# Turning the gated activations of a mixture of adapters by DMA in pairs, with two moves in the order of the work around it

## The chip, the cores and the metric

The kernel runs on one core of one Trainium2 chip. The metric is the time of one execution on the device in microseconds (us). One execution of each kernel was also recorded by the hardware profiler; its span, from the first to the last instruction of the program, is what the views of the profile divide up.

## The reference

Two layers follow one another. The first is attention with pooled keys; the second sends each row through the best two of eight low-rank adapters and adds the result to the row.

```python
B, N, C = 4, 12288, 128            # q: [4, 12288, 128], kv: [4, 384, 32, 128]
kv_pool = kv.reshape(B, H // 4, 4, W // 4, 4, C).mean(axis=(2, 4))   # 4x4 patches: 768 rows a batch
k = v = kv_pool.reshape(B, -1, C) @ w_sr
s = (q @ k.transpose(0, 2, 1)) / np.sqrt(C)
a = softmax(s)
x = (a @ v).reshape(B * N, C)
logits = x @ w_gate                 # 8 experts
topk = best 2 of 8 by logits;  w = softmax of those two logits
out = x + sum over the two e of  w_e * ((x @ A[e]) @ B[e])      # rank 16 each
```

All of it is fp32 in and out. The 8 adapters of rank 16 fill one 128 x 128 matrix side by side, so that "down" (x @ A) and "up" (@ B) are one 128 x 128 matmul each for 128 rows, with the gate (the weight of each expert, zero for six of the eight) multiplied in between.

## The kernel before

**Tiling.** The 49,152 rows are cut into 96 chunks of 512 rows (NCHUNK), 24 for each batch (NB). Four chunks form a group (GC), for which q comes in once: GpSimd's queue casts the group to bf16 into a buffer in DRAM (`cast_q`, L83), and the Sync engine's queue reads it back transposed (`load_qT`, L92), so that the channels lie on the partitions. The 768 keys of a batch are six tiles of 128 (J).

**What happens to a chunk.**
- `scores` (L309): three units of two key tiles each; two matmuls of 512 columns into `sg`, then one exponential on ScalarE into `em`.
- `attend` (the tile `acc`): for each quarter of 128 rows, six matmuls of `em` against the values. The values carry extra columns, one of them ones, so that the sums of the softmax and the logits come along. There is one buffer of `acc`.
- `normalize` (L330, L338): VectorE takes the reciprocal and multiplies; this makes `xn` and frees `acc`.
- `top` and `route` (L358 to L376) on VectorE and GpSimd, and `gates` (L383 to L386: a tanh on ScalarE, two operations on GpSimd) make the gate weights `gw`, for two chunks at a time in the main part.
- `transposes` (L407): TensorE turns `xn`, and for some chunks the gated activations of another chunk, into one PSUM tile `tt_ps`, which VectorE copies out as `tts`.
- `down` (`h_ps`), `gate` (L439, VectorE, writes `hg`, `h` or `hs`), a transpose of the gated activations, `up` (`d_ps`), and `finish` (L486, VectorE adds `xn`; every second one stores two chunks, L491, on the Sync queue).

**Slots.** The body of the loop over `k` is called a slot here. From slot 13 on, slot `k` computes the scores of chunk `k`, attends chunk `k-1`, normalizes chunk `k-2`, and lets one older chunk `x_` enter down and gate: `enter[k]` is chunk `k-4` in the main part. Every engine runs its instructions in the order in which the loop writes them (`keep`). Slots 0 to 7 are an order written out by hand.

**Three ways of turning the gated activations.** Between gate and up, the activations of a chunk must be transposed.
- By TensorE (`by_pe` and all chunks in no other list): four 128 x 128 transposes (`tt_ps<-id_bf,hg`) in the slot after the gate, and the copy L407 is twice as wide.
- Through the Sync queue (`by_queue`, chunks 9 to 65): `gate_turn` writes the gated tile, and a transposing DMA (L459) turns it; up comes six or seven slots after the gate (`up_slot`). Chunks with k % 4 == 1 go alone (tiles `h1`, `t1`, shown as `t<-h`); chunks with k % 4 == 3 and the next one share a DMA (tiles `hs`, `ht`, four buffers). Chunks with k % 4 == 2 (14, 18, ..., 62), and chunk 10, are left to TensorE.
- By strip (chunks 66 to 89, SOLO and TURN mark the bounds): one DMA (`turn_dma`, L425) turns the rows of one chunk and the gated activations of another. These are the late slots, from 74 on, with an order of their own: two units of scores, down, normalize, gate, then two quarters of `attend` with `up` and `finish` of up to two chunks, and two more quarters.

**Where the Sync queue stands.** A group's `load_qT` is written at the start of slot 4g-6, unless the chunk that enters in this slot is in `by_queue`; then it follows the DMA of `gate_turn`. For groups 6 to 18 that chunk is one with k % 4 == 2.

**Keys of the next batch.** The patches of the second batch are summed by 24 operations on GpSimd (L229 and L227), which `sums.pop(0)()` places at the end of even slots 8 to 20. The steps `keys`, `values` and `turn` of its three thirds are taken from `rest` at slots 14 to 16, 18 to 20 and 21 to 23; `keys` of the last third (tile `kpT_ps`) is in slot 21 and needs all 24.

Of the kernel before, what the change touches and what calls it, by code (L numbers as in the profile page):

```python
# [20 lines left out]
def kernel(  # L21
# [47 lines left out]
    def mm(*a, **k):  # L69
        return keep(nc.tensor.matmul(*a, **k))  # L70
# [240 lines left out]
    def attend(k, s):  # L311
        b = k // NB
        if s == 0:
            acc[k] = ps_a.tile([P, S, 256], FP32, tag="acc", name="acc")
        o = acc[k][:, s, 0:VE]
        for j in range(J):
            mm(o, em[k][:, s, j], vx[b][:, j, 0:VE], start=(j == 0),
               stop=(j == J - 1))
# [25 lines left out]
    SOLO, TURN = NCHUNK - 6, NCHUNK - 28  # L344
# [75 lines left out]
    def narrow(k, t):  # L420
        keep(nc.gpsimd.tensor_copy(strip(t, 0)[:, 0], xn[k][:, :, 0:C]))
# [14 lines left out]
    def gate(k, into=None):  # L436
        k0, m = first[k], k - first[k]
        hg[k] = run.tile([P, S, P], BF16, tag="hg", name="hg") if into is None else into
        keep(nc.vector.tensor_tensor(  # L439
            hg[k].rearrange("p s (e r) -> p (s e) r", e=E),  # L440
            hp[k].rearrange("p s (e r) -> p (s e) r", e=E),
            gw[k0][:, m * S:(m + 1) * S].rearrange("p s e -> p (s e)")
            .unsqueeze(2).broadcast_to([P, S * E, RK]), op=ALU.mult))
# [1 line left out]
    pair = []  # L445

    def gate_turn(k):
        if k % 4 == 1:
            src, dst = (hpool.tile([P, 1, S, P], BF16, tag=tag, name=tag, bufs=3) for tag in ("h1", "t1"))
        elif k % 4 == 3:  # L450
            src, dst = (hpool.tile([P, 2, S, P], BF16, tag=tag, name=tag) for tag in ("hs", "ht"))
            pair[:] = src, dst
        else:
            src, dst = pair
        i = int(k % 4 == 0)
        gate(k, src[:, i])
        hgT[k] = dst[:, i]
        if k % 4 != 3:
            keep(nc.sync.dma_start(dst.rearrange("c h s p -> c (h s) p"),  # L459
                                   src.rearrange("p h s c -> p (h s c)"), transpose=True))  # L460

# [81 lines left out]
    def begin(k):  # L543
        nonlocal sums, rest
        b, i = divmod(k, NB)
        g = k // GC
        if k in casts:
            cast_q(4 + casts.index(k))
        if k in halves:
            g, u = halves[k]  # L550
            cast_q(g, u, u + 4)
        if k in rows_at:
            load_kv(*rows_at[k], None)
        if i == 0 and 0 < b < B - 1:
            rest = prepare(b + 1, nc.gpsimd)[1]
        if k == 3:
            sums, rest = prepare(1, nc.gpsimd)
            sums = sum(sums, [])
        if 3 <= k < 15:
            load_kv(1, (k - 3) // 4, (k - 3) % 4, None)  # L560
        if k == 7:
            for _ in range(2):
                sums.pop(0)()
# [16 lines left out]
        left = [k for k in left if k not in enter[t]]  # L580
        t += 1

    by_queue = [k for k in range(9, TURN - 2) if k % 4 != 2 and k != 10]
    by_strip = range(TURN - 2, SOLO)
    slot = {x_: t for t, xs in enter.items() for x_ in xs}
    taken = [slot[x_] + (3 if x_ in by_strip else 2) for x_ in slot if x_ not in by_queue]
# [7 lines left out]
    by_pe = enter[SOLO - 2][1:]  # L594
# [14 lines left out]
    kh, ku, kd, kdone = [], [], [], []  # L609
# [40 lines left out]
    kh, ku = enter[k1 - 1], enter[k1 - 2]  # L650
    for k in range(k1, NCHUNK):
        b, i = divmod(k, NB)
        ka = att.get(k, [])
        kx = enter.get(k, [])
        begin(k)

        def after_norm(kn):
            top(kn)
            if kn == first[kn] + size[kn] - 1:
                route(first[kn])  # L660

        kn = [n for n in att.get(k - 1, []) if normed[n] == k]
        unit()
        if k in loads and k < TURN + 5 and not any(x_ in by_queue for x_ in kx):
            load_qT(loads[k])
        ku = ku + late_up.pop(k, [])
        if kx and not kd and all(x_ in by_dma for x_ in kx):
            down(kx[0])
            todo = []
            for n in kn:  # L670
                normalize(n)
                if n in by_dma:
                    narrow(n, k)
                    todo = [(xT, n)]
            tanhs()
            for h_ in kh:
                if h_ in by_pe:
                    transposes(None, h_, nc.vector)
            unit()
            gate(kx[0], strip(k, 0)[:, 1])  # L680
            todo.append((hgT, kx[0]))
            if k != SOLO + 2:
                turn_dma(k, *todo)
                if k in loads:
                    load_qT(loads[k])
            for n in range(2):
                if kh and kh[0] in by_pe:
                    attend(ka[0], n)
                if n < len(ku):
                    up(ku[n])  # L690
                    finish(ku[n])
                if not (kh and kh[0] in by_pe):
                    attend(ka[0], n)
            assert len(ku) < 3
            unit()
            for n in kn:
                after_norm(n)
            attend(ka[0], 2)
            for x_ in kx[1:]:
                down(x_)  # L700
                if x_ in by_pe:
                    gate(x_)
                elif k < SOLO - 3:
                    turn_alone(x_)
                else:
                    gate(x_, strip(k, 0)[:, 0])
                    turn_dma(k, (hgT, x_), *todo)
            attend(ka[0], 3)
            for x_ in kx:
                if x_ not in by_pe:  # L710
                    up_at(k + (3 if k < SOLO - 3 else 2), x_)
            kh, ku = [x_ for x_ in kx if x_ in by_pe], [c for c in kh if c in by_pe]
            continue
        tanhs()
        for x_ in kd:
            down(x_)
        todo = []
        for n in kn:
            normalize(n)
            if n in by_dma:  # L720
                narrow(n, k)
                todo.append((xT, n))
        px = [c for c in kx if c not in by_dma]
        ph = [c for c in kh if c not in by_queue and c not in by_strip]
        pairs = [(px[j] if j < len(px) else None, ph[j] if j < len(ph) else None)
                 for j in range(max(len(px), len(ph)))]
        for x_, h_ in pairs[:1]:
            transposes(x_, h_, nc.vector)
        for x_ in kd:
            gate(x_)  # L730
        unit()
        for u_ in ku:
            up(u_)
            finish(u_)
        for a_ in ka[:-1]:
            for s in range(S):
                attend(a_, s)
            normalize(a_)
            after_norm(a_)
        if ka and len(ka) == 1:  # L740
            attend(ka[0], 0)
        for n in kn:
            after_norm(n)
        for x_ in kx[:1]:
            down(x_)
        if k >= 13:
            unit()
            n0 = 1
        else:
            attend(ka[0], 1)  # L750
            n0 = 2
        for x_ in kx[:1]:
            if x_ in by_queue:
                gate_turn(x_)
                up_at(up_slot[x_], x_)
                if k in loads:
                    load_qT(loads[k])
            elif x_ in by_strip:
                gate(x_, strip(k, 0)[:, 1])
                turn_dma(k, *todo, (hgT, x_))  # L760
                todo = []
                up_at(k + 3, x_)
            elif k == NCHUNK - 1:
                turn_alone(x_)
                up(x_ - 1)
                finish(x_ - 1)
            else:
                gate(x_)
        if todo:
            turn_dma(k, *todo)  # L770
        kd = []
        if rest and i in ((14, 15, 16, 18, 19, 20, 21, 22, 23) if b == 0 else (5, 6, 7, 13, 14, 15, 21, 22, 23)):
            rest.pop(0)()
        for a_ in ka[-1:]:
            for s in range(n0 if len(ka) == 1 else 0, S):
                if s == S - 1:
                    for x_, h_ in pairs[1:]:
                        transposes(x_, h_, nc.scalar)
                        kd = [x_] if x_ is not None else []
                attend(a_, s)  # L780
        ku = [c for c in kh if c not in by_queue and c not in by_strip]
        kh = kx[:1] + kdone
        kdone = kd
        if k % 2 == 0 and 8 <= k <= 20:
            for _ in range(4 if k == 18 else 3):
                sums.pop(0)()
        for w in adds_at.get(k, []):
            add_patches(*w)
# [174 lines left out]
```

## Time and profile before

| what | value |
|---|---|
| three runs | 372.04, 379.13 and 382.07 us; median 379.13 us |
| the profiled execution | 371.5 us, of which the span is 369.7 us |
| TensorE matmul (PE) busy | 358.4 us, 97% of the span |
| VectorE (DVE), ScalarE (ACT), GpSimd (POOL) busy | 292.5, 292.7 and 229.8 us |
| mean granted TensorE clock | 0.999 |
| DMA | 88.08 MB, mean 238 GB/s |

PEld is TensorE's weight load, which overlaps its matmuls; SPq is the Sync engine's queue of DMA issues. In a row of the timeline the first number is the start, the second the time from the first to the last of the merged instructions, then engine, line, operation, out<-in, shapes, and a count; what stands in brackets is the idle time of the engine before the row and what ended it. The profiled execution was shorter than each of the three runs.

### The profile page before, as it was taken

The page shows a single profiled execution, that of the slowest core. Times are in us where ns is not written, and L with a number is a line of the kernel's source. Part 1 is how long each engine was busy: PE and PEld are TensorE (multiplying, and loading weights), DVE is VectorE, ACT ScalarE, POOL GpSimd, SP SyncE. Part 2 cuts the span into 40 slices and gives each one's busy share as a digit, 9 for nine tenths or more (in the row PEclk, how much of TensorE's full clock was granted, in tenths as well). Part 3 has the DMA queues.
Part 4 walks back from the last instruction along what each step waited for, and adds up shares of the span by engine and source line. Part 5 has one row for each costly group of instructions (what it writes and reads, how often), then busy time and mean ns, then how long its engine had stood idle before and what let it go on. Part 6 is the DMA issues. An engine that isn't in the chain of part 4 may idle for free.

```text
span 369.7 us, 11065 instructions
## 1 busy us (share of the span) xinstructions
PE 358.4 (97%) x4266; PEld 281.2 (76%) x4272; DVE 292.5 (79%) x923; ACT 292.7 (79%) x363; POOL 229.8 (62%) x519
## 2 busy tenths in 40 slices
PE   7999999999999999999999999999999999999993
PEld 4767788877787787787787877788787777777782
DVE  1347799887888888888898888888887777679795
ACT  1548986787878888888878878879878999898873
POOL 1110368889878677667758757766666766565442
PEclk9999999999999999999999999999999999999999
DMA  7989769999798999999999999999699999999723
GB/s 246 383 301 222 252 173 278 307 296 230 181 275 198 256 303 286 221 223 330 186 249 282 253 244 223 278 299 238 135 185 224 258 220 202 222 210 208 208 87 156
DMA packets 72869, 88.08 MB, mean 238 GB/s; under 512 B 51345, under 2 KB 51601, under 8 KB 72465
## 3 DMA queue, kind: packets, MB, share of 16 engines
q1 hardware_dynamic: 65728, 62.93, 67.8%
q0 software_dynamic: 6656, 24.12, 28.8%
q8 instruction: 33, 0.54, 0.6%
q10 hardware_dynamic: 432, 0.33, 0.3%
q14 instruction: 20, 0.16, 0.1%
HBM read 50.53 MB, written 36.70 MB: 236 GB/s over the span
## 4 chain that ended last, share of the span: by engine, by line
PE 87%; DMA 4%; DVE 3%; POOL 3%; issue 1%; ACT 1%; SPq 0%; DVEq 0%; ACTq 0%; POOLq 0%
PE acc L70 35%; PE sg L70 31%; PE d_ps L70 5%; PE tt_ps L70 5%; PE h_ps L70 5%; PE kpT_ps L70 2%; DMA kvr<-in_kv_dram 2%; DMA turn<-turn 2%; POOL kvr L229 1%; PE v_ps L70 1%; PE qT_ps L70 1%; PE kfT_ps L70 1%; DVE xn L338 1%; ACT em L309 1%; POOL kvr L227 1%
## 5 line engine op out<-in xcount | busy, mean ns | idle before, releaser
L309 ACT ACTIVATE em<-sg 128x1024 f16<-128x1024 f32 x288 | 283.1, 1022 | 58.0 <-PE sg L70 55.3
L70 PE MATMUL sg<-qT,kfT 128*128 128x512 bf16 x570 | 169.2, 379 | 0.5 <-ACT em L309 0.2
L70 PE MATMUL acc<-vx,em 128*128 128x136 f16 x2280 | 167.5, 223 | 0.3
L70 PEld LDWEIGHTS <-em 128*128 128x128 f16 x2304 | 146.6, 98 | 18.7 <-DVE xn L338 3.0
L338 DVE TENSOR_TENSOR xn<-acc,rinv 128x540 f32<-128x540 f32 x95 | 68.4, 720 | 3.3
L486 DVE TENSOR_TENSOR osb<-d_ps,xn 128x512 f32<-128x512 f32 x92 | 62.8, 688 | 2.4 <-PE d_ps L70 0.5
L541 POOL TENSOR_TENSOR kvr<-kvr 128x512 f32<-128x512 f32 (+1 forms) x48 | 57.0, 1203 | 0.5
L370 POOL TENSOR_TENSOR over<-xn,srt 128x64 f32<-128x64 f32 (+1 forms) x120 | 31.0, 279 | 36.2 <-DVE srt L358 34.4
L385 POOL TENSOR_TENSOR gw<-th,over 128x64 f32<-128x64 f32 (+1 forms) x60 | 17.3, 288 | 48.6 <-ACT th L383 48.1
L70 PEld LDWEIGHTS <-kfT 128*128 128x128 bf16 x576 | 45.2, 98 | 2.7 <-issue 0.6
L330 DVE RECIPROCAL rinv<-acc 128x4 f32<-128x4 f32 x95 | 17.3, 182 | 34.8 <-PE acc L70 32.0
L407 DVE COPY tts<-tt_ps 128x1024 bf16<-128x1024 bf16 (+1 forms) x73 | 36.8, 505 | 0.0
L70 PEld LDWEIGHTS <-xn 128*128 128x128 bf16 x296 | 22.5, 98 | 16.5 <-DVE xn L338 0.2
L358 DVE MAX8 srt<-xn 128x8 f32<-128x8 f32 x380 | 34.5, 153 | 0.1
L70 PEld LDWEIGHTS <-tts 128*128 128x128 bf16 x388 | 27.0, 98 | 7.0 <-DVE tts L407 0.4
L70 PE MATMUL h_ps<-a_bf,tts 128*128 128x128 bf16 x284 | 27.5, 219 | 0.0
L70 PE MATMUL tt_ps<-id_bf,xn 128*128 128x128 bf16 x284 | 27.4, 219 | 0.0
L376 POOL TENSOR_SCALAR over<-over 128x64 f32<-128x64 f32 (+1 forms) x60 | 19.8, 330 | 5.4
L439 DVE TENSOR_TENSOR hs<-h_ps,gw 128x512 bf16<-128x512 f32 x28 | 19.1, 683 | 4.5 <-POOL gw L386 4.0
L229 POOL TENSOR_TENSOR kvr<-kvr 128x512 f32<-128x512 f32 x18 | 22.4, 1270 | 0.1
L439 DVE TENSOR_TENSOR hg<-h_ps,gw 128x512 bf16<-128x512 f32 x26 | 17.9, 688 | 5.8 <-POOL gw L386 5.2
L70 PEld LDWEIGHTS <-turn 128*128 128x128 bf16 x176 | 13.2, 98 | 9.4 <-DMA turn<-turn 0.9
(98 smaller groups left out, 313.8 us busy)
## 6 DMA issues: line engine op xcount, KB each, us to landing
out_dram<-osb SPq DMA_DIRECT2D x46, 512.0 KB, 5.7
kvr<-in_kv_dram POOLq DMA_DIRECT2D x24, 512.0 KB, 6.8
kvr<-in_kv_dram SPq DMA_DIRECT2D x21, 512.0 KB, 7.6
qbf<-in_q_dram POOLq DMA_DIRECT2D x20, 512.0 KB, 6.8
qf<-in_q_dram SPq DMA_DIRECT2D x8, 256.0 KB, 7.5
kvr<-in_kv_dram SPq DMA_DIRECT2D x6, 256.0 KB, 7.5
qbf<-in_q_dram POOLq DMA_DIRECT2D x4, 256.0 KB, 5.5
out_dram<-osb SPq DMA_DIRECT2D x3, 256.0 KB, 2.4
```

Of the source, the lines that this page charges most:

```text
L70: return keep(nc.tensor.matmul(*a, **k))
L229: keep(adder.tensor_tensor(u[:, lo:hi], u[:, lo:hi], v[:, lo:hi], op=ALU.add))
L309: keep(nc.scalar.activation(o, i_, AF.Exp, bias=0.0, scale=scale))
L330: keep(nc.vector.reciprocal(ri, acc[k][:, :, VC]))
L338: keep(nc.vector.tensor_tensor(x[:, :, 0:VC], acc[k][:, :, 0:VC], ri.unsqueeze(2).broadcast_to([P, S, VC]), op=ALU.mult))
L358: keep(nc.vector.max(srt[k0][:, m, s], xn[k][:, s, C:C + E]))
L370: keep(eng.tensor_tensor(d, lg, so[:, :, i].unsqueeze(2).broadcast_to([P, n, 8]), op=ALU.subtract))
L376: keep(eng.tensor_scalar(mask, mask, 0.0, None, op0=ALU.is_ge))
L407: keep(nc.vector.tensor_copy(sb[:, lo:hi], ps[:, lo:hi]))
L439: keep(nc.vector.tensor_tensor(hg[k].rearrange("p s (e r) -> p (s e) r", e=E), hp[k].rearrange("p s (e r) -> p (s e) r", e=E), gw[k0][:, m ...
L486: keep(nc.vector.tensor_tensor(osb[:, int(k == kb)], dp[k], xn[k][:, :, 0:C], op=ALU.add))
L541: keep(nc.gpsimd.tensor_tensor(u, u, v, op=ALU.add))
```

## The change

Three things change. All chunks from 11 to 65 go through the Sync queue, and two neighbours, odd and even, share one transposing DMA; only 9 and 65 go alone. Their up comes seven slots after the gate (six from chunk 56 on), and `load_qT` in slots 18, 22, ..., 66 now follows the DMA of the slot's pair. One of GpSimd's sums moves from slot 18 to slot 16 and one from slot 20 to slot 18. And in the late slots a quarter of `attend` is always written ahead of each `up`.

```diff
     def gate_turn(k):
-        if k % 4 == 1:
+        alone = k % 2 and k + 1 not in by_queue
+        if alone:
             src, dst = (hpool.tile([P, 1, S, P], BF16, tag=tag, name=tag, bufs=3) for tag in ("h1", "t1"))
-        elif k % 4 == 3:
+        elif k % 2:
             src, dst = (hpool.tile([P, 2, S, P], BF16, tag=tag, name=tag) for tag in ("hs", "ht"))
             pair[:] = src, dst
         else:
             src, dst = pair
-        i = int(k % 4 == 0)
+        i = int(k % 2 == 0)
         gate(k, src[:, i])
         hgT[k] = dst[:, i]
-        if k % 4 != 3:
+        if alone or i:
             keep(nc.sync.dma_start(dst.rearrange("c h s p -> c (h s) p"),
                                    src.rearrange("p h s c -> p (h s c)"), transpose=True))
...
-    by_queue = [k for k in range(9, TURN - 2) if k % 4 != 2 and k != 10]
+    by_queue = [k for k in range(9, TURN - 2) if k != 10]
...
             for n in range(2):
-                if kh and kh[0] in by_pe:
-                    attend(ka[0], n)
+                attend(ka[0], n)
                 if n < len(ku):
                     up(ku[n])
                     finish(ku[n])
-                if not (kh and kh[0] in by_pe):
-                    attend(ka[0], n)
...
         if k % 2 == 0 and 8 <= k <= 20:
-            for _ in range(4 if k == 18 else 3):
+            for _ in range(4 if k in (16, 18) else 2 if k == 20 else 3):
                 sums.pop(0)()
```

## The prediction

> **What bounds the kernel now.** I read the page first, then the windows by stage, the groups of TensorE's instructions in the main part, the timeline of two neighbouring slots, and last the Sync queue, GpSimd and the late slots. The page says that TensorE has next to nothing to give away:
>
> ```profile
> span 369.7 us, 11065 instructions
> PE 358.4 (97%) x4266; PEld 281.2 (76%) x4272; DVE 292.5 (79%) x923; ACT 292.7 (79%) x363; POOL 229.8 (62%) x519
> ```
>
> A busy TensorE need not be one that sets the time, so look at starts rather than busy time. Two slots of the main part, the second with the gated activations turned by TensorE:
>
> ```profile
> 169.35 1.23 PE L70 MATMUL acc<-vx,em 128*128 128x136 f16 x18
> ...
> 171.07 0.59 PE L70 MATMUL sg<-qT,kfT 128*128 128x512 bf16 x2
> ...
> 172.73 1.23 PE L70 MATMUL acc<-vx,em 128*128 128x136 f16 x18
> ...
> 174.23 0.39 PE L70 MATMUL tt_ps<-id_bf,xn 128*128 128x128 bf16 x4
> 174.45 0.39 PE L70 MATMUL tt_ps<-id_bf,hg 128*128 128x128 bf16 x4
> 174.68 0.59 PE L70 MATMUL sg<-qT,kfT 128*128 128x512 bf16 x2
> ...
> 176.34 1.23 PE L70 MATMUL acc<-vx,em 128*128 128x136 f16 x18
> ```
>
> From `acc` to `acc` the first slot takes 172.73 - 169.35 = 3.38 us, the second 3.61. The difference, 0.23, is just the time from the `hg` transposes to the next matmul (174.68 - 174.45). So a slot is as long as what TensorE issues in it, and four transposes cost 0.23 us of the end.
>
> **Part 1: 13 chunks leave TensorE.** Chunks 14, 18, ..., 62 are 13, so 52 transposes go. The group in the stretch 100 to 276 us is the thing removed (48 matmuls, which is 12 chunks; the 13th is just ahead of the stretch):
>
> ```profile
> L70 PE MATMUL tt_ps<-id_bf,hg 128*128 128x128 bf16 x48 | 4.6, 219 | 0.0
> ```
>
> Its busy time counts overlapping matmuls twice over; 0.23 for each chunk is the price. For the 12, 12 x 0.23 = -2.8 us; the 13th falls into a stall of part 2 and is counted there. VectorE's copy gets shorter as well, worth nothing while TensorE sets the pace. Bounds: -2.8, and 0 if another engine takes over.
>
> What is added: as many transposing DMAs as before (15 single and 14 pairs become 2 and 27), but 13 more chunks in them. The queues show what this meets:
>
> ```profile
> 124.00:166.00 42.00, 42.00 (x519) 33.28 (x517) 36.57 (x117) 34.44 (x42) 29.63 (x57) 1.00 1.11 258
> ```
> ```profile
> 171.88 3.45 SPq L92 DMA_TRANSPOSE qT<-qbf  x1
> 173.17 0.69 DVE L439 TENSOR_TENSOR hg<-h_ps,gw 128x512 bf16<-128x512 f32 x1 [0.27 <-POOL gw L386]
> ...
> 209.25 1.25 SPq L459 DMA_TRANSPOSE ht<-hs  x1
> ...
> 213.90 7.06 SPq L92 DMA_TRANSPOSE qT<-qbf  x1
> ...
> 234.15 0.59 PE L70 MATMUL sg<-qT,kfT 128*128 128x512 bf16 x2
> ```
> ```profile
> DMA to landing us min/median/max: 3.1/4.0/6.9
> ```
> ```profile
> DMA to landing us min/median/max: 11.7/11.7/11.7
> ```
>
> The last two are the pairs (`ht`), and the load of q issued at 213.90. In the first row the column before the last is the DMA share: 1.11, packets overlapping, no room to see. A pair has 2 chunks and lands at best 3.1 us after its issue, 1.25 of which is the issue: (3.1 - 1.25) / 2 = 0.93 us of the DMA engines for a chunk, an upper estimate. The Sync queue also gets a new order: `load_qT` of groups 6 to 18 stood at the start of the slot and now stands behind the gate and the pair's DMA. In the slot above that gate ended at 173.86, and with 1.25 for the issue the load starts at 175.1 instead of 171.9, 3.2 us later; the next store and pair queue up behind its long issue, but their own users are some slots away. The load at 213.90, the tightest I found, landed at 225.6; its group's first scores start at 234.15, so 8.5 us of cover. Less 3.2, less 0.93 for one more chunk directly ahead, leaves 4.4 us. Up comes six slots after the pair's DMA, about 20 us, against 4 to 7 us for landing; and the four pair buffers come round after eight slots, one slot after the last up that reads them. I take 0 for the DMAs, covered by these 4.4 us; the bounds are 0 and what the second rival works out.
>
> The Trainium skill says in Advanced Engine Details and Errata, X-Bar Transpose (TRN2), that such DMAs run about as fast as plain ones, 350 to 400 GB/s. By that a chunk of 128 KiB would be an estimated 0.35 us, not 0.93, and the DMA side of this change would hardly exist; the row decides.
>
> **Part 2: sums of the second batch.** In slots 16 to 21 GpSimd works without a break:
>
> ```profile
> 82.05 1.27 POOL L229 TENSOR_TENSOR kvr<-kvr 128x512 f32<-128x512 f32 x1
> ...
> 84.97 0.36 POOL L376 TENSOR_SCALAR over<-over 128x64 f32<-128x64 f32 x1
> ...
> 86.12 0.32 POOL L385 TENSOR_TENSOR gw<-th,over 128x64 f32<-128x64 f32 x1 [0.24 <-ACT th L383]
> 86.79 4.95 POOL L229 TENSOR_TENSOR kvr<-kvr 128x512 f32<-128x512 f32 x4
> 86.87 0.69 DVE L439 TENSOR_TENSOR hg<-h_ps,gw 128x512 bf16<-128x512 f32 x1 [1.01 <-POOL gw L386]
> 87.48 0.41 DVE L251 TENSOR_SCALAR kpT<-kpT_ps 128x256 f32<-128x256 f32 x1
> 88.03 0.72 DVE L338 TENSOR_TENSOR xn<-acc,rinv 128x540 f32<-128x540 f32 x1
> 88.81 0.46 PEld L70 LDWEIGHTS <-em 128*128 128x128 f16 x6 [0.21 <-DVE xn L338]
> 95.83 2.07 POOL L227 TENSOR_TENSOR kvr<-kvr 128x512 f32<-128x512 f32 x2
> 97.02 0.59 PE L70 MATMUL sg<-qT,kfT 128*128 128x512 bf16 x2
> 97.96 0.44 PE L70 MATMUL kpT_ps<-id_f,kvr 128*128 128x128 f32 x2 [0.35 <-POOL kvr L227]
> ```
>
> The wait that the move aims at is the last row: two score matmuls hold TensorE for 0.44 us (293.80 to 294.24, below), so it could go on at about 97.46 and starts `kpT` at 97.96, 0.5 us. But moving a sum ahead does not shorten a line in which nothing idles: before the last sum GpSimd idled 0.24. What the move does is to put 1.27 us ahead of `over`, hence ahead of the tanh and of `gw`. The gate in slot 18 already waits 1.01 us for `gw` and then runs at 86.87; it would run at about 87.95. On VectorE the copy L251, the reciprocal and `xn` queue behind it: 87.95 + 0.69 + 0.41 + 0.2 + 0.72 = 89.97. `attend` needs `xn` done, since `acc` has one buffer, and already waits 0.21 for it at 88.81; it would start at 90.03, +1.2 us (the 0.23 of chunk 14's transposes, gone here, vanishes in this wait). From there all of GpSimd and TensorE stand 1.1 to 1.2 later alike, the last sums end at about 97.7, TensorE arrives at 98.6, and the 0.5 is gone. Sum: +1.2 - 0.5 = +0.7. Bounds: -0.5, if the later gate is hidden, and +1.2.
>
> **Part 3: a quarter of attend ahead of up.** Two late slots, the first without an up, the second with one:
>
> ```profile
> 290.51 0.72 DVE L338 TENSOR_TENSOR xn<-acc,rinv 128x540 f32<-128x540 f32 x1
> 290.74 0.59 PE L70 MATMUL sg<-qT,kfT 128*128 128x512 bf16 x2
> 291.29 0.88 PE L70 MATMUL acc<-vx,em 128*128 128x136 f16 x12
> ...
> 293.57 0.72 DVE L338 TENSOR_TENSOR xn<-acc,rinv 128x540 f32<-128x540 f32 x1
> 293.80 0.59 PE L70 MATMUL sg<-qT,kfT 128*128 128x512 bf16 x2
> 294.24 0.39 PE L70 MATMUL d_ps<-b_bf,turn 128*128 128x128 bf16 x4
> 294.46 0.87 PE L70 MATMUL acc<-vx,em 128*128 128x136 f16 x12
> ...
> 296.51 0.18 DVE L330 RECIPROCAL rinv<-acc 128x4 f32<-128x4 f32 x1 [0.75 <-PE acc L70]
> ```
> ```profile
> 316.95 0.40 PE L70 MATMUL d_ps<-b_bf,turn 128*128 128x128 bf16 x4 [0.42 <-DMA turn<-turn]
> ```
>
> Up is what TensorE does while VectorE still reads `acc`. In the second slot TensorE is free at 294.24, `xn` ends at 294.29, up fills 0.22 and `acc` starts without a wait. In the first there is nothing to fill with: `xn` ends at 291.23, `acc` starts 0.06 later, at 291.29, 0.11 after TensorE was free (290.74 + 0.44). With attend ahead every such slot is like the first: +0.11. Slots 74, 75, 77 to 88 and 90 to 92 are 17, so 17 x 0.11 = +1.9 us. `finish` comes 0.46 later on VectorE, inside the 0.75 it idles before the reciprocal. In return the one wait for a turned tile, 0.42, is hidden by the six matmuls now ahead of it: -0.4. Sum +1.5; bounds -0.4 and +1.9.
>
> **The sum.** -2.8 + 0.7 + 1.5 = -0.6 us against the profiled execution's 371.5 (span 369.7): 370.9 us, no change to speak of. That execution lies below all three runs and 7.6 us below their median of 379.13; if the changed kernel's runs scatter alike, their median may lie as far above, which the range has to hold. Its own bounds: -2.8 - 0.5 - 0.4 = -3.7 and -2.8 + 1.2 + 1.9 = +0.3, so 367.8 to 371.8.
>
> **The rivals.**
> 1. All that was moved is hidden: 371.5 - 3.7 = 367.8 us. For it, the waits it takes away are real rows; against it, the 0.11 and the 1.01 are rows too. 0.12.
> 2. The DMA engines become the bound, the slower side. In the full stretch, some 124 to 250 us, nine of the 13 chunks are added, 9 x 0.93 = 8.4 us, while TensorE runs 9 x 0.23 = 2.1 us ahead: by the end the transfers are 10.5 us late. It decides from the point where the load of q for a group has used up its 4.4 us; then the first scores of a group wait for `qT`. 10.5 - 4.4 = 6.1, so 377.0 us; with no cover at all 381.4. Against it: 0.93 is an upper estimate, and the median pair lands in 4.0 us, hardly over its best of 3.1, in this same stretch. 0.24, of which 0.20 is slower by over 2%, since runs with slower transfers would pass 379. The Trainium skill speaks for it in DMA: Bandwidth & Descriptors, Issuing engines are not separate DMA queues: what the Sync and GpSimd queues start shares the same 16 engines, so that turned tiles also hold up casts and key loads; no row here shows the two apart.
> 3. The three runs are longer than the profiled one because waits like the 0.42 at 316.95 are many and long in them, and attend ahead hides them: then the changed kernel's runs come out near 370 against 379.13, faster by 2.4%. No row shows such a run. 0.14.
> 4. It does not free what it says, because ScalarE takes the pace:
> ```profile
> L309 ACT ACTIVATE em<-sg 128x1024 f16<-128x1024 f32 x288 | 283.1, 1022 | 58.0 <-PE sg L70 55.3
> ```
> Three such exponentials a slot are 3.07 us of 3.38 before any tanh. Then the 2.8 are not gained: 370.9 + 2.8 = 373.7. Slots of 3.38 us without these transposes exist, which speaks against it. 0.05.
>
> **How the numbers follow.** Forecast 0.45, rivals 0.12, 0.24, 0.14, 0.05. Over 2% (about what a measurement of this kernel can tell from no change): faster 0.14, from rival 3; slower 0.20 + 0.02 from rivals 2 and 4 = 0.22; the same 0.64. The range goes from 367.0, under rival 1, to 380.5, nearly the end of rival 2.
>
> **What would show it.** Right: no `tt_ps<-id_bf,hg` after slot 15; slots of 3.38 us where there were 3.61; a wait of about 1 us for `xn` near 89 us and none at `kpT` in slot 21; `acc` in late slots 0.1 us behind TensorE's readiness with a wait for `xn`, these slots 0.11 us longer. Wrong: waits of `sg` for `qT` (rival 2), or late slots as long as before.

## The result, and the profile after

The changed kernel takes 391.24 us in the median of six runs (387.85 to 397.07), the kernel before 376.19 us in six (371.84 to 382.07). The ratio is 1.0476, 95% interval 1.0422 to 1.0529: slower by 4.8%, while the forecast was 370.9 us, in a range of 367.0 to 380.5. The ratio is taken only from the executions of each kernel that lie within 1.5% of its fastest; the profiled one took 395.48 us (span 393.6), is longer than these, and is set against the 371.5 of before, so that the 24.0 us between the two are more than those 4.8%.

The page, and from the view of waits those in which TensorE waits for q:

```profile
span 393.6 us, 10970 instructions
PE 366.0 (93%) x4220; PEld 281.3 (71%) x4220; DVE 290.7 (74%) x923; ACT 294.0 (75%) x363; POOL 230.3 (58%) x519
```
```profile
PE sg L70 <- DMA qT<-qbf: 14.8, 4, 5.2
```

TensorE has 46 matmuls fewer on record and is busy for longer (366.0 us instead of 358.4), yet for a smaller share of the span, 93% instead of 97%. Four times the scores wait for a load of q, 14.8 us in all, at most 5.2; before there is no such wait. One of them in the timeline of TensorE:

```profile
148.80 1.23 PE L70 MATMUL acc<-vx,em 128*128 128x136 f16 x18
155.10 1.04 PE L70 MATMUL sg<-qT,kfT 128*128 128x512 bf16 x2 [5.08 <-DMA qT<-qbf]
...
156.36 1.06 PE L70 MATMUL sg<-qT,kfT 128*128 128x512 bf16 x2
...
161.37 0.59 PE L70 MATMUL sg<-qT,kfT 128*128 128x512 bf16 x2
```

Between two such rows of `sg` at the start of slots lie 3.38 us elsewhere; here, from 155.10 to 161.37, lie 6.27, after the wait is over and with nothing idle. Two score matmuls take 1.06 instead of 0.59. The stretch 156 to 159 us says why; the number that follows the five engines, 0.50, is the granted clock:

```profile
156.00:159.00 3.00, 3.00 (x22) 2.35 (x21) 1.40 (x6) 2.19 (x3) 1.37 (x3) 0.50 1.20 179
```

TensorE runs at half its clock for some microseconds after the wait: 2.9 us more. Three of the four waits are of this kind (5.08, 5.17 and 3.82 us); the fourth, 0.74 us, is followed by rows of the usual length.

The Sync queue around the second wait, and the time to landing of the pairs and of the loads of q, all of the changed kernel:

```profile
182.61 1.28 SPq L460 DMA_TRANSPOSE ht<-hs  x1
183.98 16.52 SPq L92 DMA_TRANSPOSE qT<-qbf  x1
200.59 0.53 SPq L492 DMA_DIRECT2D out_dram<-osb  x1
```
```profile
DMA to landing us min/median/max: 3.1/9.3/18.2
```
```profile
DMA to landing us min/median/max: 4.3/8.6/21.6
```

The load is in its place, right behind its pair, but the queue needs 16.52 us to issue it, where 7.16 was the longest before, and the pairs take a median of 9.3 us instead of 4.0. The load lands 21.6 us after the start of its issue, at 205.6, just when the second wait ends (205.61). GpSimd's queue, in which the change puts nothing, is slower too. These are its loads of keys, before and after; the last number is the median time to landing:

```profile
kvr<-in_kv_dram POOLq DMA_DIRECT2D x24, 512.0 KB, 6.8
```
```profile
kvr<-in_kv_dram POOLq DMA_DIRECT2D x24, 512.0 KB, 10.4
```

The stretch from 124 to 250 us, first of before, then of after; the last two columns are the DMA share and GB/s:

```profile
124.00:250.00 126.00, 126.00 (x1561) 100.20 (x1559) 108.86 (x341) 104.16 (x124) 89.90 (x170) 1.00 1.09 260
```
```profile
124.00:250.00 126.00, 114.35 (x1349) 89.36 (x1346) 93.66 (x300) 91.98 (x109) 80.45 (x151) 0.96 1.09 234
```

The share is the same, 1.09, and the rate is lower, which fits DMA engines that had been full already before. An account of the 24.0 us from these rows: 14.8 of waits for q; 1.7 to 3.1 of low clock behind each of three of them, 7.7 in all (the slots around these waits are 21.8 us longer than slots of 3.38, of which 14.1 are the waits); about +2.0 in the late slots (17 of 0.12, below); about +0.4 from the sums; -2.8 for the transposes gone. That is 22.1; a wait of 0.7 for a pair and a start 0.5 us later bring it to 23.3, and 0.7 I do not place.

### The profile page after: what moved, and what is told of

The parts are those of the page before. It is cut to its first block, busy times and chain, and to the rows that moved or that the text cites. A ratio compares the mean times of both kernels' runs of the same rounds, so it can differ in the third digit from the quotient of the medians.

```text
span 393.6 us, 10970 instructions
## 1 busy us (share of the span) xinstructions
PE 366.0 (93%) x4220; PEld 281.3 (71%) x4220; DVE 290.7 (74%) x923; ACT 294.0 (75%) x363; POOL 230.3 (58%) x519
## 3 DMA queue, kind: packets, MB, share of 16 engines
q1 hardware_dynamic: 69056, 64.63, 70.8%
## 4 chain that ended last, share of the span: by engine, by line
PE 65%; DMA 24%; POOL 4%; DVE 3%; issue 1%; ACT 1%; SPq 0%; DVEq 0%; ACTq 0%; POOLq 0%
PE acc L70 27%; PE sg L70 24%; DMA qT<-qbf 16%; PE d_ps L70 4%; PE h_ps L70 4%; DMA kvr<-in_kv_dram 4%; PE tt_ps L70 4%; POOL kvr L229 2%; DMA qf<-in_q_dram 2%; DMA turn<-turn 2%; DVE xn L338 1%; PE v_ps L70 1%; PE kpT_ps L70 1%; ACT em L309 1%; POOL kvr L227 0%
## 5 line engine op out<-in xcount | busy, mean ns | idle before, releaser
L70 PE MATMUL sg<-qT,kfT 128*128 128x512 bf16 x576 | 174.0, 386 | 15.2 <-DMA qT<-qbf 14.8
L70 PE MATMUL acc<-vx,em 128*128 128x136 f16 x2280 | 172.4, 225 | 0.9 <-DVE xn L338 0.9
L70 PEld LDWEIGHTS <-em 128*128 128x128 f16 x2304 | 148.7, 99 | 28.2 <-DVE xn L338 11.9
L407 DVE COPY tts<-tt_ps 128x512 bf16<-128x512 bf16 (+1 forms) x73 | 33.2, 454 | 16.3 <-PE tt_ps L70 16.3
L439 DVE TENSOR_TENSOR hs<-h_ps,gw 128x512 bf16<-128x512 f32 x54 | 36.9, 683 | 10.0 <-POOL gw L386 8.6
L70 PE MATMUL tt_ps<-id_bf,xn 128*128 128x128 bf16 x284 | 28.2, 223 | 0.4 <-DVE hs L439 0.4
L70 PEld LDWEIGHTS <-ht 128*128 128x128 bf16 x216 | 17.1, 101 | 14.1 <-issue 1.7
L70 PEld LDWEIGHTS <-tts 128*128 128x128 bf16 x336 | 23.5, 99 | 3.5 <-DVE tts L407 0.2
L70 PE MATMUL d_ps<-b_bf,ht 128*128 128x128 bf16 x216 | 21.6, 224 | 0.7 <-DMA ht<-hs 0.7
## 6 DMA issues: line engine op xcount, KB each, us to landing
kvr<-in_kv_dram POOLq DMA_DIRECT2D x24, 512.0 KB, 10.4
```

The lines of the kernel that those rows point to most:

```text
L407: keep(nc.vector.tensor_copy(sb[:, lo:hi], ps[:, lo:hi]))
L439: keep(nc.vector.tensor_tensor(hg[k].rearrange("p s (e r) -> p (s e) r", e=E), hp[k].rearrange("p s (e r) -> p (s e) r", e=E), gw[k0][:, m ...
```

## The experiments

The theory after this: the DMA engines have no time for the added chunks (throughput). Its rival: the load of q comes too late in the Sync queue's new order (order). Unless said otherwise a ratio is to the kernel before on the same chip, with its 95% interval.

**Which part.** The first: part 1 alone, the two other parts as before.

```diff
-                attend(ka[0], n)
+                if kh and kh[0] in by_pe:
+                    attend(ka[0], n)
                 if n < len(ku):
                     up(ku[n])
                     finish(ku[n])
+                if not (kh and kh[0] in by_pe):
+                    attend(ka[0], n)
...
-            for _ in range(4 if k in (16, 18) else 2 if k == 20 else 3):
+            for _ in range(4 if k == 18 else 3):
```

> Part 1 alone: all chunks from 11 to 65 by the Sync queue in pairs, the sums and the late slots as before. Both theories of the slowdown put it here: 18 to 24 us over the kernel before, with four or so waits of the scores for qT of 4 to 5 us each, as in the changed kernel. If the slowdown came from part 3 or from all three together, this would be within 4 us of before.

Its runs are 388.1, 395.54 and 408.06 us, before on this chip 372.5 in the median: part 1 alone brings a slowdown of the size of the whole change's. A fourth execution, the profiled one, took 971.86 us, with TensorE busy for 99% of it; its cause is open, and it is left out, so part 1 alone has no profile that can be read here.

The second: the kernel before with the line of the sums changed, nothing else.

```diff
-            for _ in range(4 if k == 18 else 3):
+            for _ in range(4 if k in (16, 18) else 2 if k == 20 else 3):
```

> Part 2 alone. My own step said +0.7 us (between -0.5 and +1.2): the gate of slot 18 about 1 us later, no wait for the sums at kpT in slot 21. Rival: the earlier sums save their 0.5 us and nothing else.

373.26 us, ratio 0.9998 (0.9966 to 1.0030): no change that can be told from none. Its trace shows the gate and the `attend` that I had in mind:

```profile
88.26 0.69 DVE L439 TENSOR_TENSOR hg<-h_ps,gw 128x512 bf16<-128x512 f32 x1 [2.04 <-POOL gw L386]
90.18 0.35 PEld L70 LDWEIGHTS <-em 128*128 128x128 f16 x6 [0.63 <-DVE xn L338]
98.35 0.59 PE L70 MATMUL sg<-qT,kfT 128*128 128x512 bf16 x2
98.79 0.39 PE L70 MATMUL kpT_ps<-id_f,kvr 128*128 128x128 f32 x2
```

The gate waits 2.04 us for `gw` instead of 1.01, `attend` waits for `xn` longer, and `kpT` follows the scores without a wait. By the slots' starts the stall costs 1.0 us and the relief is 0.6: +0.4 of the forecast +0.7. Unlooked for, the same execution has this, far from the edit, in a kernel with not one chunk more in its DMAs:

```profile
240.23 1.03 PE L70 MATMUL sg<-qT,kfT 128*128 128x512 bf16 x2 [4.28 <-DMA qT<-qbf]
```

It took 380.81 us. So a wait for q can occur without any chunk added, and such an execution takes some 380 us.

The third: the kernel before with `attend` ahead of `up` in every late slot.

```diff
-                if kh and kh[0] in by_pe:
-                    attend(ka[0], n)
+                attend(ka[0], n)
                 if n < len(ku):
...
-                if not (kh and kh[0] in by_pe):
-                    attend(ka[0], n)
```

> Part 3 alone. My own step said +1.5 us: every late slot with an up 0.11 us longer (3.27 for 3.16), the one wait for a turned tile hidden. Rival: the slots stay at 3.16 and the time does not move or falls.

373.01 us, ratio 1.0009 (0.9975 to 1.0043), which neither excludes the +1.5 nor shows it. The slots do show it; two of them in the changed kernel:

```profile
330.30 0.53 PE L70 MATMUL acc<-vx,em 128*128 128x136 f16 x6
330.67 0.39 PE L70 MATMUL d_ps<-b_bf,turn 128*128 128x128 bf16 x4
...
333.05 0.59 PE L70 MATMUL sg<-qT,kfT 128*128 128x512 bf16 x2
333.59 0.53 PE L70 MATMUL acc<-vx,em 128*128 128x136 f16 x6
```

From `acc` to `acc` 3.29 us, against 3.17 before (291.29 to 294.46 there), and 0.54 from `sg` to `acc` where 0.44 is the time of the scores. The trace of this run, part 3 alone, has the same 3.29 (294.55 to 297.84). The forecast 0.11 a slot stands. That trace, of an execution of 380.31 us, also has a wait of 2.42 us for a pair, and in a late slot (305.72) one of 1.01 for a turned tile, though the forecast had such a wait hidden by the matmuls now ahead of it.

**Order or throughput.** Part 1 alone, with the load of q at the start of its slot again:

```diff
-            if k in loads and k < TURN + 5 and not any(x_ in by_queue for x_ in kx):
+            if k in loads and k < TURN + 5:
                 load_qT(loads[k])
...
                 up_at(up_slot[x_], x_)
-                if k in loads:
-                    load_qT(loads[k])
```

> Part 1 alone, with the load of q put back to the start of its slot, ahead of the pair's DMA. Theory of order (the load starts 3 us late, behind a store and two chunks): the waits for qT vanish and the time is 2 to 3 us under before. Theory of throughput (the DMA engines have no time for 13 more chunks, in whatever order): waits of the same sum, over 10 us, on qT or on the turned pairs, and the time at least 8 us over before.

395.01 us, ratio 1.0549 (1.0450 to 1.0648), no better at all. The waits have changed their object:

```profile
PE d_ps L70 <- DMA ht<-hs: 15.3, 6, 4.6
```

15.3 us, now for the pairs, where it had been 14.8 for q. What stands behind in the queue is late. The converse, the kernel before with its load of q moved behind the gate and no chunk added:

```diff
-            if k in loads and k < TURN + 5 and not any(x_ in by_queue for x_ in kx):
+            if k in loads and k < TURN + 5 and not any(x_ in by_queue or x_ in range(14, 63) for x_ in kx):
...
                 gate(x_)
+                if k in loads and x_ in range(14, 63):
+                    load_qT(loads[k])
```

> The kernel before with nothing changed but the place of the load of q: in slots 18 to 66 it stands behind the gate of the entering chunk, as in the changed kernel, some 3 us later, with no chunk added to the DMAs. If that lateness alone did harm, several us slower; by my 8.5 us of cover, no change (within 1%).

373.38 us, ratio 1.0009 (0.9968 to 1.0051). The order alone makes no difference that can be told from none, as the cover of 8.5 us said.

**How many chunks.** Part 1 for 7 of the 13:

```diff
-    by_queue = [k for k in range(9, TURN - 2) if k != 10]
+    by_queue = [k for k in range(9, TURN - 2) if k % 8 != 2]
```

> Part 1 for 7 of the 13 chunks (14, 22, ..., 62); 18, 26, ..., 58 stay with TensorE, and their odd neighbours go alone as before. Throughput: the lateness grows with the chunks added, so the time lies between, 3 to 12 us over before, with one or two waits for qT or a pair. A threshold that is crossed only by all 13: at or under before (7 x 0.23 = 1.6 us under).

Four runs: 369.88, 381.2, 382.72 and 386.51 us. One is near where a kernel with 7 x 0.23 us less for TensorE should be; three are 8 to 14 us above the 372.91 of before. Only the longest was profiled; it has this wait, and another idle stretch of TensorE of 4.68 us, at 162.80, for which its profile names no cause:

```profile
232.23 1.04 PE L70 MATMUL sg<-qT,kfT 128*128 128x512 bf16 x2 [6.58 <-DMA qT<-qbf]
```

As far as four runs tell, the time does not grow evenly with the chunks; what grows is how often an execution is a long one. Only the last three, 54, 58 and 62:

```diff
-    by_queue = [k for k in range(9, TURN - 2) if k != 10]
+    by_queue = [k for k in range(9, TURN - 2) if (k % 4 != 2 or k >= 54) and k != 10]
```

> Part 1 for the last three of the 13 chunks alone (54, 58, 62), which are turned when the loads of keys have ended and the DMA engines have idle time; sums and late slots as before. Throughput: 3 x 0.23 = 0.7 us under before, no wait for qT or a pair added. If any added chunk in the queue is harmful: 3 us or more over before.

380.59 us against 379.33 of before on this chip, where long runs were frequent; ratio 1.0004 (0.9915 to 1.0093). Inconclusive: 0.7 us cannot be seen in this, and its profiled execution of 383.01 us has one wait of 8.60 us for q at 257. Nor does its premise hold: in the kernel before, the last load of keys is issued at 238.8 us, the load of q of slot 58, in which chunk 54 is turned, already at 228.4, and the DMA share is still 1.09 from 230 to 250 us. The other way, the kernel before with seven chunks of the full stretch taken out of the queue:

```diff
-    by_queue = [k for k in range(9, TURN - 2) if k % 4 != 2 and k != 10]
+    by_queue = [k for k in range(9, TURN - 2) if k % 4 != 2 and k != 10 and not (k % 4 == 1 and 29 <= k <= 53)]
```

> The dose turned the other way: the kernel before with seven chunks (29, 33, ..., 53) taken out of the queue and turned by TensorE, 7 x 0.23 = 1.6 us more for TensorE and seven chunks less for the DMA engines in their full stretch. If the kernel before already stands at the limit of its DMA engines, which would make its own runs of 379 us and more, the runs here lie within 3 us of each other, near 373.5, none at 379 or more. If those long runs have another cause, they are as frequent here, and every run is 1.6 us longer.

374.08 us, ratio 1.0059 (1.0026 to 1.0092), so +2.2 us for the forecast +1.6; and its 12 runs lie between 372.83 and 376.64, while the 17 of before beside it reach 390.16, three of them above 380. That fits the theory without proving it: if three long runs fell at random on these 29, none would be among the 12 about one time in five. Its share in the stretch:

```profile
124.00:250.00 126.00, 126.00 (x1573) 100.67 (x1571) 109.70 (x337) 103.87 (x123) 88.68 (x167) 1.00 1.03 252
```

**Which cost.** Part 1 alone without 27 of the stores:

```diff
-        if n % 2:
+        if n % 2 and not 11 <= kb <= 65:
```

> Part 1 alone, and the 27 stores of pairs of chunks with the later one from 11 to 65 are left out, so these rows of the output are not written: 512 KB less for the DMA engines every second slot. If the engines lack time in total, the waits for qT and the pairs vanish and the time falls to 368 to 371 us, 2 to 4 under before. If the transposing DMAs are slow by themselves (their 256-byte packets, or a limit of their own), waits of over 5 us stay.

368.95 us, ratio 0.9870 (0.9782 to 0.9959), and no wait for q or for a pair. And part 1 alone with DMAs that copy in place of turning:

```diff
-            keep(nc.sync.dma_start(dst.rearrange("c h s p -> c (h s) p"),
-                                   src.rearrange("p h s c -> p (h s c)"), transpose=True))
+            keep(nc.sync.dma_start(dst.rearrange("c h s p -> c (h s p)"),
+                                   src.rearrange("p h s c -> p (h s c)")))
```

> Part 1 alone, with the DMAs of gate_turn copying their tile as it lies instead of turning it (so the up of these chunks multiplies values in the wrong order): the same bytes, in rows of 1 or 2 KB instead of 256-byte pieces. If it is the pieces that cost, the waits vanish: 368 to 371 us. If it is the bytes or the number of DMAs, the time stays near 388 to 395.

369.39 us, ratio 0.9876 (0.9802 to 0.9950), no such wait either. Each relief alone is enough, so it is the sum of the work that is too much, and not a limit of the turning by itself. Both reliefs act on the Sync queue, and no run takes work from another queue alone, so whether the sum that counts is that of the 16 DMA engines or that of this one queue is not separated. GpSimd's loads of keys speak for the engines: they land in a median of 10.4 us in the changed kernel, 6.4 without the stores and 7.2 with plain copies.

That the form of a transfer counts, and not only its bytes, is in the Sync queue's line of the page (packets, MB, share of 16 engines' span), in the changed kernel and here:

```profile
q1 hardware_dynamic: 69056, 64.63, 70.8%
```
```profile
q1 hardware_dynamic: 43632, 64.63, 62.7%
```

The same 64.63 MB: 0.708 x 393.6 = 278.7 us of the engines with turning, 0.627 x 367.4 = 230.4 without. For the 56 chunks of the queue that is 0.86 us a chunk more, but part of it is delay and not work: the run with the sums alone moved has the transfers of before, and its line says 70.4% of 379.0 us, 266.8, where the profiled execution of before has 250.7. The two runs without waits give the better price. A turned chunk is 512 packets of 256 bytes. In the packet records of the kept traces, the packets of this size take 98.5 us of the engines in the run without stores, and 43.5 in the run with plain copies, where those of the 56 chunks are gone: 55.0 us, or 0.98 a chunk. The larger packets of the same chunks, copied as they lie, take about 20 us there, some 0.4 a chunk. And the stretch, without stores and with plain copies:

```profile
124.00:250.00 126.00, 126.00 (x1554) 100.00 (x1552) 108.10 (x347) 105.22 (x127) 91.15 (x173) 1.00 0.94 193
```
```profile
124.00:250.00 126.00, 126.00 (x1554) 100.02 (x1552) 108.09 (x347) 105.23 (x127) 91.14 (x173) 1.00 0.97 269
```

In these profiles shares of 0.94, 0.97 and 1.03 go without waits for q or a pair, and so does the 1.09 of before, while the 1.09 of the changed kernel goes with 14.8 us of waits for q. So the share shows that there is no room left, but not how late the transfers are. The plain copies move 269 GB/s at 0.97, the changed kernel 234 at 1.09.

**What a wait costs.** The kernel before, with one gap put into TensorE's work in slot 63, a long one, shown, and a short one (`range(0)` for `range(3)`); the scratch tiles `hold_f` and `hold` are made ahead of the loop:

```diff
+        if k == 63:
+            for _ in range(3):
+                keep(nc.gpsimd.tensor_tensor(hold_f, hold_f, hold_f, op=ALU.add))
+            keep(nc.gpsimd.tensor_copy(hold, hold_f[:, 0:P]))
+            mm(mtile([P, T], name="spin_ps"), hold, zero, start=True, stop=True)
```

> The kernel before, with TensorE made to wait once in slot 63 for GpSimd (three additions and a copy on a scratch tile, then one extra matmul), a gap of some 5 to 6 us as long as the waits for qT in the changed kernel. If a wait of this length also lowers TensorE's granted clock for some us after it, as the slots behind the waits suggest, the time grows by the gap and 2 to 3 us more, 7 to 9 in all, in a run without other waits. Rival: the long slots behind the waits come from the DMAs, and the time grows by the gap alone, 5 to 6.

> The same with the copy alone: a gap of some 2 us. With the clock theory a short gap brings no lower clock: the time grows by the gap, about 2 us. Rival: it grows by the gap and 2 to 3 us here too.

```profile
250.94 0.39 PE L70 MATMUL spin_ps<-zero,hold 128*128 128x512 bf16 x1 [4.25 <-POOL hold L670]
251.17 0.98 PE L70 MATMUL sg<-qT,kfT 128*128 128x512 bf16 x2
...
254.94 0.59 PE L70 MATMUL sg<-qT,kfT 128*128 128x512 bf16 x2
```
```profile
250.90:253.90 3.00, 2.96 (x16) 1.77 (x17) 0.69 (x1) 1.03 (x2) 0.00 (x0) 0.56 1.01 227
```
```profile
256.28 0.39 PE L70 MATMUL spin_ps<-zero,hold 128*128 128x512 bf16 x1 [1.42 <-POOL hold L670]
256.50 0.59 PE L70 MATMUL sg<-qT,kfT 128*128 128x512 bf16 x2
...
258.62 0.59 PE L70 MATMUL sg<-qT,kfT 128*128 128x512 bf16 x2
```

The first two fences are the long gap, the third the short one; the same work lies between the two rows of `sg`. Behind a gap of 4.25 us it takes 254.94 - 251.17 = 3.77 us, with a granted clock of 0.56 in these 3 us; behind one of 1.42 us it takes 2.12. So the long gap costs 1.65 more than itself, the short one nothing. The time of the long gap, 379.66 us, ratio 1.0158 (1.0077 to 1.0239), is +5.9 us, in line with 4.25 + 1.65, but the interval, 2.9 to 8.9 us, does not exclude the gap alone; the rows decide. I had expected a gap of 5 to 6 and 2 to 3 of low clock, so both were smaller. The short gap's runs (373.48 to 385.5) give no verdict, since the profiled one has 7.8 us of waits for q elsewhere; its rows do. Neither gap is a wait for a DMA.

The length of the stall is not all that counts, as two waits for pairs in the run with the load first show, one of 2.47 us that ends at 187.63 and one of 3.26 us that ends at 200.07. The stretches of 3 us behind them:

```profile
187.60:190.60 3.00, 2.96 (x21) 2.52 (x22) 1.66 (x6) 0.74 (x1) 2.02 (x3) 0.58 0.76 231
200.00:203.00 3.00, 2.93 (x40) 2.46 (x41) 1.95 (x8) 1.02 (x1) 1.27 (x2) 1.00 1.65 335
```

The shorter one is followed by a clock of 0.58, the longer one by the full clock. What decides between them is open.

## Why the prediction was wrong

**The step that failed** is in part 1: "I take 0 for the DMAs, covered by these 4.4 us". The prediction read the share of 1.11 as full, and then charged nothing for work added to a full resource. In its place the runs showed 14.8 us of waits for q and 7.7 of low clock behind them, and neither where the same chunks were copied instead of turned. The 4.4 us were reckoned for one load with one chunk more ahead of it, but the lateness grew from load to load: the four up to the first wait took 9.8, 12.6, 11.8 and 15.3 us to land, those of the same slots before 8.9, 8.9, 10.4 and 10.0. What was charged with this price was the second rival, at 0.24, with 377.0 us, or 381.4 with no cover. It names what happened, and its sign was seen, the waits of `sg` for `qT`; but the kernel takes 391.24.

**What the rival had right and wrong.** Its price held: 0.93 us a chunk, from a pair at its best, against 0.98 in the two runs without waits. The Sync queue's packets took 0.678 x 369.7 = 250.7 us before (its line on the page below) and 278.7 after; these 28.0 us, 2.2 for each of 13 chunks, are not that price, since delay alone moved this figure by 16 us in the run with the sums moved.

```profile
q1 hardware_dynamic: 65728, 62.93, 67.8%
```

Its cover did not hold. The 4.4 us were taken from one execution that had no wait. The kernel before has long executions too, three of 17 above 380 us beside the lessened dose; none of these was profiled, but in near copies of it profiled executions of this length hold a wait for q (4.28 us) or for a pair (2.42 us): the cover was at times already used up. The waits for q came to 14.8 us, where the rival reckoned the transfers 10.5 late.

And it had no term for the clock: a stall of 3.8 to 5.2 us cost TensorE a further 1.7 to 3.1 us at half clock, 7.7 in the profiled execution. The Trainium skill has this in TensorE: Matmul & The Clock Gate, What's actually happening: the clock halves after an idle window of some 3.4 us and comes back after about as much activity. The rows agree with it behind 5.08 us (0.50), 4.25 (0.56), 3.26 (1.00) and 1.42 (no longer rows), but not behind 2.47, which is shorter than that window and was followed by 0.58. The rivals charged a wait with its own length alone.

The remark beside the price, by the Trainium skill in Advanced Engine Details and Errata, X-Bar Transpose (TRN2), that a turned chunk should cost an estimated 0.35 us, does not hold here: that is about what the plain copy took (some 0.4), and turning took 0.98.

**What held.** TensorE's gain in part 1 is real: with the DMAs relieved (no stores, plain copies) the times are 368.95 and 369.39, 3.5 to 4 us under the 372.91 of before, and rival 4, ScalarE as the bound, is excluded. The order of the load alone did no harm that can be seen, as its cover said. Part 2 came out as +0.4 for +0.7, by the steps given. Part 3's 0.11 a slot is 0.12 in the trace, and is lost in the noise of whole runs.

**Rival 3** had it right that the long runs of before go with waits for DMAs, as far as the profiles of near copies show. But the larger of these are in the full stretch (4.28 us for q at 240, 2.42 for a pair at 246) and not in the late slots, and attend ahead of up does not remove them: with part 3 alone, three of 11 runs are longer than 380 us.

## What to carry to other kernels

When a view shows a resource full, work moved onto it has to be charged in full from the first microsecond, whatever cover single transfers seem to have; ask what it moves per microsecond at that share, and by which form of transfer. Executions of one kernel that scatter by 2 to 3% are a reading too: in near copies of this kernel the longer ones held waits for DMAs before any work was added, and with seven chunks taken off the queue none of 12 was long, at a price of 2.2 us. Add the clock to the price of a stall of TensorE. Of the versions tried here, only the two that skip part of the work came out clearly under the kernel before.

## What the runs showed of the hardware

- Turning tiles by DMA cost the DMA engines more than copying the same bytes: 0.98 us for a chunk of 128 KiB in packets of 256 bytes, some 0.4 as a plain copy.
- Moving the load of q forward in the queue only moved the waits from q to the pairs (14.8 against 15.3 us).
- Stalls of TensorE of 3.82 to 5.17 us, for DMAs and once for GpSimd, were followed by some microseconds at half clock, which cost 1.7 to 3.1 us more; one of 1.42 us was not. In between, one of 2.47 us was followed by a low clock and one of 3.26 us was not.
